# A gated block on one NeuronCore: gate and up of two of four chunks by seven block products in place of eight

## The chip, the cores and the metric

The kernel runs on one core of one Trainium2 chip. Its time is device microseconds of one execution, the median of several runs. The engines have a queue each and work it in order: TensorE (matmuls, in the profile PE, its weight loads PEld), VectorE (DVE), ScalarE (ACT), GpSimd (POOL); SyncE (SP) issues the DMAs. TensorE writes to banks of PSUM, each of 128 partitions by 512 f32 values, and the banks are read by VectorE and ScalarE.

## The reference

For 2048 rows of width 576 (f32):

```python
xn = layernorm(x)
# A: attention, 32 heads of width 18, causal, a window of 256
q, k, v = split(xn @ wqkv)
s = softmax(mask(q @ k.T * 18 ** -0.5)) @ v  @ wo
# B: bilinear gated unit, inner width 4608, no nonlinearity inside
g = silu(((xn @ w_gate) * (xn @ w_up)) @ w_down)
out = x + s * g
```

The kernel keeps f32 accuracy with f16 matmuls: each operand is split into a high and a low f16 part (high = f16(scaled value), low = the rest), and a product is high x high + high x low + low x high.

## The kernel before

**The data.** `XT` holds the normalized x transposed, 128 partitions by nine planes by 2048 columns: planes 0 to 3 are the high parts of the 512 first rows of D, plane 4 the high part of the last 64 rows (partitions 0 to 63) and their low part (64 to 127), planes 5 to 8 the low parts. `XT2` repeats the high part of the last 64 rows in partitions 64 to 127. One tile of weights (`UW[g, k]`, ten planes of 128 x 128) has the high parts of four full blocks and the tail in planes 0 to 4, the low ones in 5 to 9. In plane 4 the 64 last rows stand twice, so that a single pass there gives high x high and high x low of the tail.

**The order of the work.** After a prologue of some 180 us (layernorm, q, k, v) come 72 slots: 18 groups `g` of 256 inner columns (two tiles `ft` of 128), and in each the four chunks `c` of 512 rows. A slot is `sl = 4 * g + c` and has 16 places. In each place TensorE gets a quarter of a gate or up product: gate of ft 0 at places 0 to 3, up of ft 0 at 4 to 7, then ft 1. A product is 13 passes of 512 columns and one half-row pass for low x high of the tail; a gate's and an up's half-row pass run side by side in the two halves of the rows (lines 933 and 934).

All else is put between them by a table written out by hand: `at(slot, place, f, ...)`; a place of 16 or more falls into a later slot. In each place first the matmuls of gate and up are issued (with `gate_out` or `up_out` at the last quarter), then the score matmuls, then the down matmuls, then the rest in the order in which it was put in the table. Each engine works this order as it comes, so an operation that waits holds what stands behind it on its engine.

- **FFN.** `gate_out` (line 773, ScalarE) copies the gate's bank to `gt`, `up_out` (778, VectorE) multiplies the up bank by it into `ht`. `h_hi` (783, ScalarE) and `h_lo` (788, VectorE) split it. `down` (801) is eight groups of six matmuls of 288 columns a slot, each added to `acc` by VectorE (806); the eight take turns on one bank, `dn`, at places 7, 9, 11, 13, 15, 17, 19, 21 after their slot's start plus one slot.
- **Attention**, one pair of heads a slot, in slots 1 to 64. `score_pairs` (678, TensorE, places 3 and 11), `score` (686, VectorE: masks and takes the maximum), line 688 (GpSimd: the bias of the exponential), `probs` (693 and 696, ScalarE: exponential and high part), `turn_probs` (701: the low part, j = 0 on VectorE, j = 1 on GpSimd, and then a DMA transpose from SP, 704), `weigh` (713, TensorE, 37 columns) in the next slot, `finish` (725 to 737, VectorE and GpSimd) and `store_o` (742) every sixteen steps.
- **Weights.** For each group, `ffn_raw` loads the next group's weights; `ffn_amax` takes maxima on VectorE, `ffn_spread_out` and `ffn_spread_in` bring them to all partitions over DRAM, `ffn_scale` makes scales; `up_hi` (147, ScalarE), `up_lo` (150, VectorE) and `dn_hi`, `dn_lo`, `dn_low` (413, GpSimd) make the parts. In steady state chunk 0 has the gate's maxima and two `dnw` parts, chunk 1 the other maxima, chunks 2 and 3 the scale and the parts.

PSUM's eight banks are four `s`, two `up`, one `dn`, one `pv`. A gate and an up bank are allocated together every eight places.

## Time and profile before

| | |
|---|---|
| median of 3 runs | 1644.06 us (1643.51 to 1644.07) |
| the profiled execution's own time | 1644.22 us |
| its span, first to last instruction | 1642.5 us |
| TensorE busy | 1632.9 us, 99% |
| VectorE, ScalarE, GpSimd busy | 1182.4, 912.0, 608.0 us |
| a slot of the steady part | 19.83 us |

In a row of the profile's groups stand line, engine, operation, what it writes and reads by the program's names, its shape and count, then busy time and mean ns of one, then the idle time of the engine ahead of it and what ended it. In the view of busy time by windows, each row is a stretch of the run, with the busy time of every engine. In a timeline a row has start, length, engine, line, operation and count; matmuls are pipelined and their ends modelled, so that their starts tell the rate.

### The profile page before, as it was taken

What the parts mean: (1) busy time and instruction counts of PE and PEld (TensorE: products, weight loads), DVE (VectorE), ACT (ScalarE), POOL (GpSimd) and SP (SyncE); (2) the same over time, 40 slices, a digit from 0 to 9 for tenths busy, and PEclk for the clock granted to TensorE, in tenths of its full rate; (3) what the DMA queues carried; (4) which work ended last, traced back from release to release, by engine and by line L of the source; (5) the groups of instructions that cost most, each with busy time, mean ns of one, the idle gap of its engine ahead of it and who ended that gap; (6) DMA issues with size and microseconds to landing.
All of it is one profiled execution on the core that took longest, in us unless ns stands there. A gap on an engine that the chain in (4) does not pass through costs nothing.

```text
span 1642.5 us, 33722 instructions
## 1 busy us (share of the span) xinstructions
PE 1632.9 (99%) x12330; PEld 931.7 (57%) x12330; DVE 1182.4 (72%) x2993; ACT 912.0 (56%) x1581; POOL 608.0 (37%) x1044
## 2 busy tenths in 40 slices
PE   8999999999999999999999999999999999999999
PEld 5464455555555555555555555555555555555577
DVE  7533577777677878787878787878787877865545
ACT  6431465656565656676666666666666666632230
POOL 3110134434343545454444444444444453511000
PEclk9999999999999999999999999999999999999999
DMA  9571446455556777676767575767665766650228
GB/s 241 160 199 74 127 86 118 97 109 109 107 107 131 144 120 136 113 144 114 142 137 144 109 147 103 152 105 145 139 136 114 142 118 129 129 130 20 60 70 219
DMA packets 531798, 206.37 MB, mean 126 GB/s; under 512 B 470576, under 2 KB 510384, under 8 KB 531632
## 3 DMA queue, kind: packets, MB, share of 16 engines
q1 hardware_dynamic: 531632, 204.21, 60.3%
q8 instruction: 97, 1.59, 0.4%
q14 instruction: 69, 0.57, 0.1%
HBM read 76.63 MB, written 23.75 MB: 61 GB/s over the span
## 4 chain that ended last, share of the span: by engine, by line
PE 97%; DMA 1%; ACT 0%; DVE 0%; issue 0%; POOL 0%; SPq 0%; POOLq 0%; DVEq 0%; ACTq 0%
PE up L930 49%; PE dn L801 24%; PE pv L713 4%; PE s L337 3%; PE up L933 3%; PE s L678 2%; PE s L801 2%; PE s L895 2%; PE up L895 1%; PE up L337 1%; PE s L288 1%; PE pv L337 1%; PE dn L337 1%; DMA xr<-in_A_x_dram 0%; PE up L288 0%
## 5 line engine op out<-in xcount | busy, mean ns | idle before, releaser
L930 PE MATMUL up<-XT,upw 128*128 128x512 f16 x3744 | 926.6, 378 | 0.0
L930 PEld LDWEIGHTS <-upw 128*128 128x128 f16 x3744 | 331.0, 97 | 279.6 <-issue 0.8
L801 PE MATMUL dn<-dnw,hh 128*128 128x288 f16 x3168 | 475.6, 286 | 0.0
L801 PEld LDWEIGHTS <-hh 128*128 128x128 f16 x3456 | 326.2, 98 | 198.9 <-issue 41.1
L806 DVE SCALAR_TENSOR_TENSOR acc<-dn,sc,acc 128x288 f32<-128x288 f32 x496 | 255.9, 516 | 248.9 <-PE dn L801 243.0
L688 POOL TENSOR_SCALAR mx<-mx,sig 128x1 f32<-128x1 f32 x512 | 199.7, 390 | 529.9 <-DVE mx L686 500.0
L713 PEld LDWEIGHTS <-pt 128*128 128x128 f16 x2880 | 138.1, 96 | 57.9
L713 PE MATMUL pv<-vt,pt 128*128 128x37 f16 x2880 | 142.9, 179 | 0.0
L773 ACT ACTIVATE gt<-up 128x512 f32<-128x512 f32 x144 | 85.4, 593 | 83.9 <-PE up L933 80.1
L783 ACT ACTIVATE hh<-ht 128x512 f16<-128x512 f32 x144 | 89.9, 624 | 60.8 <-DVE ht L778 60.8
L778 DVE SCALAR_TENSOR_TENSOR ht<-up,gt 128x512 f32<-128x512 f32 x144 | 99.1, 688 | 21.0 <-PE up L930 8.5
L788 DVE SCALAR_TENSOR_TENSOR hh<-hh,ht 128x512 f16<-128x512 f16 x144 | 98.8, 686 | 0.0
L375 DVE TENSOR_REDUCE am<-raw 128x1 f32<-128x640 f32 (+1 forms) x108 | 85.0, 787 | 0.9 <-DMA raw<-in_B_w_gate_dram 0.9
L413 POOL TENSOR_SCALAR dnw<-dnw 128x576 f16<-128x576 f16 x36 | 69.1, 1919 | 23.1 <-ACT dnw L147 20.4
L147 ACT ACTIVATE upw<-raw,sc 128x640 f16<-128x640 f32 x72 | 59.0, 823 | 23.3 <-DVE sc L126 22.3
L337 PEld LDWEIGHTS <-upw 128*128 128x128 f16 x416 | 40.4, 98 | 49.5 <-issue 1.7
L150 DVE SCALAR_TENSOR_TENSOR upw<-raw,sc,upw 128x640 f16<-128x640 f32 x72 | 62.9, 876 | 0.1
L678 PE MATMUL s<-ks,qs 54*128 54x384 f16 (+2 forms) x512 | 60.2, 312 | 0.0
L933 PE MATMUL up<-XT,upw 64*128 64x512 f16 x144 | 55.7, 387 | 0.0
L934 PE MATMUL up<-XT,upw 64*128 64x512 f16 x144 | 55.7, 387 | 0.0
L895 PEld LDWEIGHTS <-ot 128*128 128x128 f16 x476 | 44.5, 98 | 10.7
L806 DVE SCALAR_TENSOR_TENSOR acc<-s,sc,acc 128x288 f32<-128x288 f32 x48 | 24.6, 517 | 35.4 <-PE s L801 35.3
(2248 smaller groups left out, 2193.6 us busy)
## 6 DMA issues: line engine op xcount, KB each, us to landing
raw<-in_B_w_down_dram SPq DMA_DIRECT2D x36, 288.0 KB
qk_d<-qp SPq DMA_DIRECT2D x18, 512.0 KB
raw<-in_B_w_gate_dram SPq DMA_DIRECT2D x36, 256.0 KB
raw<-in_B_w_up_dram SPq DMA_DIRECT2D x36, 256.0 KB
vt<-v_d SPq DMA_DIRECT2D x48, 111.0 KB
ks<-qk_d SPq DMA_DIRECT2D x96, 54.0 KB
v_d<-vo SPq DMA_DIRECT2D x16, 296.0 KB
xr<-in_A_x_dram SPq DMA_DIRECT2D x16, 288.0 KB
```

Source lines behind the costliest of these rows:

```text
L337: nc.tensor.matmul(ps, a, b, start=i == 0 and not opened, stop=i == 12 and opened)
L678: nc.tensor.matmul(ps[:, :hi_ - lo_], QS[s][r, i * 128:(i + 1) * 128], KS[s][r, lo_:hi_], start=True, stop=True)
L688: nc.gpsimd.tensor_scalar(mx[:, 1:2], mx[:, 0:1], sig[:, 1:2], shift, op0=OP.mult, op1=OP.add)
L713: nc.tensor.matmul(PVB[s][:, j, i, :VW], pt[:, 2 * nb * j + n], VT[s][:, lo_ + n % nb, j * VW:(j + 1) * VW], start=n == 0, stop=n == 2 * n ...
L778: nc.vector.scalar_tensor_tensor(h, ps, U_SC, GT.pop((sl, ft)), op0=OP.mult, op1=OP.mult)
L783: nc.scalar.activation(hh[:, 0], h, AF.Copy, scale=1.0 / LO)
L788: nc.vector.scalar_tensor_tensor(hh[:, 1], hh[:, 0], -LO, h, op0=OP.mult, op1=OP.add)
L801: nc.tensor.matmul(ps[:, :HALF], a, b, start=q == 0, stop=q == len(l) - 1)
L806: nc.vector.scalar_tensor_tensor(d, ps[:, :HALF], SC[g][:, 9:10], d, op0=OP.mult, op1=OP.add)
L895: nc.tensor.matmul(pr[j][:, :cols[j].stop - cols[j].start], a, b[:, cols[j]], start=i == 0, stop=i == 13)
L930: nc.tensor.matmul(banks[up], a, b, start=i == 0 and not up, stop=i == 12 and up == 1)
L933: nc.tensor.matmul(banks[0], *half_pass(w, c, False), start=False, stop=True)
```

## The change

In chunks 0 and 1 of each group from g = 1 on (34 of 72 slots) the gate and up products are computed in another way. The 512 full rows of D, the 256 inner columns of the group and the 512 rows of the chunk make a product of 2 x 2 by 2 x 2 blocks: weights `b[k, f]` (k: half of D, f: inner tile), x's `a(i, j)` (i: half of the chunk's rows, j: half of D). In place of the eight block products there are seven, from sums of x's blocks and sums of weight blocks (the Winograd form of Strassen's scheme). Each is taken with the same three passes of high and low parts, for two blocks of 128 rows each, gate and up side by side in one bank of 2 x 256 columns: 12 matmuls of 256 columns. The tail of 64 rows is added in the products 1, 4, 5 and 6, as 12 more and as four half-row ones (`seven_half`). Product 6 takes a difference of the tails (`XD`).

What is added:

- once, in slots 0 to 2: the sums of x (`s_steps`, `SUMS_AT`), about 13 GpSimd operations for each of the two chunks, with splits on ScalarE and VectorE; block (1, 0) of `XT` is overwritten by one;
- for each group: four sums of weight blocks for the gate and four for the up (`t_sum`, GpSimd), their high parts (`t_hi`, four on ScalarE) and low parts (`t_lo`, four on VectorE);
- for each of the 34 slots: three copies of banks on ScalarE (products 0, 3, 4), four reads with addition on VectorE (1, 2, 5, 6), three sums of 512 on GpSimd, and gate x up as four halves of 256 columns, three on GpSimd, one on VectorE.

In these slots `gate_out` and `up_out` are gone; `h_hi` and `h_lo` go to places 16, 17 and 17, 21. Two of the four j = 0 subtractions of `turn_probs` go from VectorE to GpSimd there. The two `up` banks take the products in turn, seven to a slot.

What is moved: the maxima, `ffn_spread_out`, `ffn_scale`, low parts of up and the `dnw` parts by some places; `finish` one place earlier behind such a slot; `store_o` writes a quarter of the head pairs each fourth step, in two or three DMAs, where it wrote four DMAs each sixteenth. Scales by powers of two change (XS, PROJ, G_SC, U_SC, and FTOP for the FFN weights), and tiles change pools so that the new ones fit: `hh`, `gt`, `ht` and `acc` in one pool in the prologue's memory (`gt` with four buffers, `ht` two), the sums in another, which closes ahead of the last two slots.

```diff
-        return ring.tile([128, 2, 512], F16, name="hh", bufs=4)
+        return post.tile([128, 2, 512], F16, name="hh", bufs=4)
     def f_ring(name):
-        return ring.tile([128, 512], F32, name=name, bufs=1)
+        return post.tile([128, 512], F32, name=name, bufs=4 if name == "gt" else 2)
...
+    SEVEN = (0, 1)
+    def seven(sl):
+        return sl >= NCH and sl % NCH in SEVEN
+    def t_sum(g, kind, pair, i):
...
+        nc.gpsimd.tensor_tensor(t[:, i], x0, x1, op=OP.subtract)
+    def t_hi(g, kind, pair):
...
+        hi(w, TF[g, kind, pair], SC[g][:, 6 + kind:7 + kind])
+    def t_lo(g, kind, pair):
...
+        lo(w[:, :, 1], TF[g, kind, pair], SC[g][:, 6 + kind:7 + kind], w[:, :, 0])
...
+        def split(n, parts):
+            return (lambda: nc.scalar.copy(parts()[0], t[n]),
+                    lambda: nc.vector.tensor_tensor(parts()[1], t[n], parts()[0], op=OP.subtract))
...
+            begin,
+            lambda: do("v", (1, 0, 1), (1, 1, 1), s),
+            lambda: do("u", "u", "v", s),
+            split("u", lambda: part(0)),
+            lambda: do("u", "u", (0, 0, 0), m),
+            lambda: do("u", "u", (0, 0, 1), m),
+            split("u", lambda: part(1)),
...
-        (nc.gpsimd if j else nc.vector).tensor_tensor(pp[:, a + n:a + 2 * n], sm, pp[:, a:a + n], op=OP.subtract)
+        (nc.gpsimd if j or seven(s + 1) and i in (0, 1) else nc.vector).tensor_tensor(pp[:, a + n:a + 2 * n], sm, pp[:, a:a + n], op=OP.subtract)
...
-        at(b, 28, finish, s)
-        if s % 16 == 15:
-            for i in range(4):
-                at(b, 33 + 4 * i, store_o, s // 16, i)
+        at(b, 27 if seven(b) else 28, finish, s)
+        if s % 4 == 3:
+            for part in range(3 if s % 16 == 15 else 2):
+                at(b, 30 + 2 * part, store_o, s // 16, s % 16 // 4, part)
...
-                    at(b, ((9, 13) if g == 1 else (5, 9), (17, 21), (24, 26))[kind][half], ffn_amax, g, kind, half)
-            at(b, 28, ffn_spread_out, g)
+                    at(b, ((9, 13) if g == 1 else (9, 9), (17, 23), (24, 29))[kind][half], ffn_amax, g, kind, half)
+            at(b, 30, ffn_spread_out, g)
             at(b, 34, ffn_spread_in, g)
-            at(b, 41, ffn_scale, g)
-            for k, (ph, pl) in enumerate(((42, 45), (47, 49), (51, 53), (55, 57))):
+            at(b, 40, ffn_scale, g)
+            for k, (ph, pl) in enumerate(((42, 45), (44, 50), (49, 53), (55, 57))):
...
+        if g > 0:
+            for n in range(4):
+                at(b, (38, 39, 40, 41)[n], t_sum, g, 0, n // 2, n % 2)
+                at(b, (51, 51, 53, 54)[n], t_sum, g, 1, n // 2, n % 2)
+            for n in range(4):
+                at(b, (45, 48, 54, 57)[n], t_hi, g, n // 2, n % 2)
+                at(b, (47, 49, 55, 58)[n], t_lo, g, n // 2, n % 2)
-        for k, (ph, pw, pl) in enumerate(((60, 62, 61), (64, 66, 66)) if g else ((64, 65, 66), (68, 69, 70))):
+        for k, (ph, pw, pl) in enumerate(((61, 62, 63), (63, 66, 65)) if g else ((64, 65, 66), (68, 69, 70))):
...
+    SUMS_AT = ((0, 1, 1, 8, 9, 10, 12, 15, 15, 19, 23, 23, 25, 26, 27, 31, 27),
+               (6, 6, 6, 11, 12, 14, 16, 17, 18, 24, 29, 29, 31, 33, 35, 40, 39))
...
+    def seven_unit(g, c, q):
+        for kind in range(2):
+            w1, w2, tw = UW[g, kind], UW[g, 2 + kind], TW[g, kind]
...
+            for n in range(2):
+                for a, b in ((wh, xh), (wh, xl), (wl, xh)):
+                    yield kind, a[:, n], b[:, n]
...
+    def seven_half(g, c):
+        CH[5], CH["n"] = bank("up", 2), 2
+        for kind in range(2):
...
+            nc.tensor.matmul(CH[4][:, o], w[0:64, 9], x[0:64], start=False, stop=kind == 1)
...
+            nc.tensor.matmul(CH[5][:, o], w[64:128, 9], xh, start=kind == 0, stop=False)
...
+    def seven_copy(sl, q, name):
+        nc.scalar.activation(seven_new(sl, name), CH[q], AF.Copy, scale=H_SC)
+    def seven_add(sl, q, x, name):
+        x = SV[sl, x]
+        nc.vector.scalar_tensor_tensor(seven_new(sl, name), CH[q], H_SC, x, op0=OP.mult, op1=OP.add)
+    def seven_sum(sl, x, y, name):
...
+        nc.gpsimd.tensor_tensor(seven_new(sl, name), x, y, op=OP.add)
+    def seven_mult(sl, name, i, f, eng):
...
+        eng.tensor_tensor(HT[sl, f][:, 256 * i:256 * i + 256], u[:, 0:256], u[:, 256:512], op=OP.mult)
+    def seven_place(sl, place):
...
+        n = SEVEN_N[place]
+        for _ in range(n):
+            q, (kind, a, b) = CH["l"].pop(0)
+            if q not in CH:
+                CH[q] = bank("up", 2)
...
+            nc.tensor.matmul(CH[q][:, o], a, b, start=CH["n"] == 0, stop=last and q != 4)
+            CH["n"] += 1
+            if last and q != 4:
+                seven_read(sl, q, place)
+        if place == 11:
+            seven_half(g, c)
+            seven_read(sl, 4, place)
...
+        elif q == 4:
+            seven_copy(sl, 4, "4")
+            at(sl, place + 1, seven_u4, sl)
+            at(sl, place + 3, seven_mult, sl, "4", 1, 1, gp)
+        elif q == 5:
+            seven_add(sl, 5, "3", "11")
+            at(sl, place + 1, seven_mult, sl, "11", 1, 0, gp)
+        else:
+            seven_add(sl, 6, "t", "t")
+            at(sl, place + 1, seven_mult, sl, "t", 0, 1, vec)
...
+    SEVEN_N = (4, 9, 7, 6, 4, 5, 6, 8, 3, 6, 3, 5, 8, 8, 8, 6)
...
+            if sl < NSLOT and seven(sl):
+                seven_place(sl, place)
+            elif sl < NSLOT:
```

189 lines of the change are left out of this document (161 added, 28 removed).

## The prediction

> **What bounds the kernel now.** I read the page first: busy time by engine, the chain that ended last, the groups (count, then busy us and mean ns, then idle before).
>
> ```profile
> PE 1632.9 (99%) x12330; PEld 931.7 (57%) x12330; DVE 1182.4 (72%) x2993; ACT 912.0 (56%) x1581; POOL 608.0 (37%) x1044
> ...
> PE 97%; DMA 1%; ACT 0%; DVE 0%; issue 0%; POOL 0%; SPq 0%; POOLq 0%; DVEq 0%; ACTq 0%
> ...
> L773 ACT ACTIVATE gt<-up 128x512 f32<-128x512 f32 x144 | 85.4, 593 | 83.9 <-PE up L933 80.1
> L783 ACT ACTIVATE hh<-ht 128x512 f16<-128x512 f32 x144 | 89.9, 624 | 60.8 <-DVE ht L778 60.8
> L778 DVE SCALAR_TENSOR_TENSOR ht<-up,gt 128x512 f32<-128x512 f32 x144 | 99.1, 688 | 21.0 <-PE up L930 8.5
> L788 DVE SCALAR_TENSOR_TENSOR hh<-hh,ht 128x512 f16<-128x512 f16 x144 | 98.8, 686 | 0.0
> ...
> L150 DVE SCALAR_TENSOR_TENSOR upw<-raw,sc,upw 128x640 f16<-128x640 f32 x72 | 62.9, 876 | 0.1
> ```
>
> The chain is TensorE's for 97% of the span. So a shorter TensorE program shortens the run, as long as the other queues keep up. How much room they have is read by stage: four neighbouring slots of the steady part (chunks 1, 2, 3, 0), from the view of busy time by windows.
>
> ```profile
> 814.44:834.27 19.83, 19.83 (x163) 11.24 (x161) 15.98 (x42) 11.71 (x20) 7.31 (x15) 1.00 0.75 130
> 834.27:854.10 19.83, 19.83 (x163) 11.23 (x161) 14.65 (x41) 12.42 (x21) 8.32 (x17) 1.00 0.79 152
> 854.10:873.93 19.83, 19.83 (x163) 11.24 (x161) 16.02 (x41) 14.31 (x24) 9.53 (x15) 1.00 0.65 135
> 873.93:893.76 19.83, 19.83 (x163) 11.24 (x161) 16.56 (x42) 12.48 (x21) 11.68 (x18) 1.00 0.80 158
> sum 79.32, PE 79.32 PEld 44.95 DVE 63.20 ACT 50.92 POOL 36.85; mean PE 19.83 PEld 11.24 DVE 15.80 ACT 12.73 POOL 9.21
> ```
>
> Columns after the length: PE, PEld, DVE, ACT, POOL, then the granted clock (1.00, full). A slot takes 19.83 us and TensorE never pauses; VectorE has 16 us a group of four free, GpSimd 42, ScalarE 28.
>
> **TensorE's term.** Its rate is read from starts, since ends are modelled. TensorE's timeline of one slot:
>
> ```profile
> 799.95 1.03 PE L930 MATMUL up<-XT,upw 128*128 128x512 f16 x4
> ...
> 802.50 1.46 PE L930 MATMUL up<-XT,upw 128*128 128x512 f16 x6
> 803.79 0.90 PE L801 MATMUL dn<-dnw,hh 128*128 128x288 f16 x6
> 804.53 1.03 PE L930 MATMUL up<-XT,upw 128*128 128x512 f16 x4
> 805.39 0.31 PE L713 MATMUL pv<-vt,pt 128*128 128x37 f16 x6
> 805.54 0.81 PE L930 MATMUL up<-XT,upw 128*128 128x512 f16 x3
> ...
> 807.08 1.46 PE L930 MATMUL up<-XT,upw 128*128 128x512 f16 x6
> 808.47 0.39 PE L933 MATMUL up<-XT,upw 64*128 64x512 f16 x1
> 808.47 0.39 PE L934 MATMUL up<-XT,upw 64*128 64x512 f16 x1
> 808.69 0.49 PE L678 MATMUL s<-ks,qs 54*128 54x384 f16 x4
> ```
>
> Six of 512 columns: 803.79 - 802.50 = 1.29, 215 ns each. Six of 288: 0.74, 123 ns. Six of 37: 0.15, 25 ns, each with its own 128x128 weights. The line through 512 and 288 gives 0.413 ns a column and 110 ns for 256 columns; half of 215 gives 107.5, the lower end. Six full ones before a half-row pair take 1.39 (807.08 to 808.47), 0.10 more than six alone: the switch of row groups.
>
> A slot now spends on gate and up 52 x 215 = 11.2 us, two half-row pairs 0.43, and two switches 0.2. Changed, it has 96 matmuls of 256 columns (seven products of 12, plus 12 for the tail rows: the sixteen entries of the new place table sum to 96), two pairs of half that length (0.22), and again two switches, one at the pairs, one at the scores of place 3, which lose the pair ahead of them. 96 x 109.5 = 10.5 us. Saved: 11.63 - 10.73 = 0.90 us a slot, or 1.08 if 107.5 holds. I take 0.91 (288 columns is the nearer row). It applies in 17 groups x 2 chunks = 34 slots: 31 us, and 37 at the other end. The slot becomes 18.9 us.
>
> The Trainium skill ("TensorE: Matmul & The Clock Gate", Back-to-back issue gap) gives a gap of N/2.4 + 2.5 ns, 109 ns here, but also says that a stream of weight-load and matmul pairs runs slower, at about 81 ns for N = 128. That speaks against halving the columns: 25 ns on each of 96 would be 2.4 us a slot, more than is saved. The 25 ns row above, weights included, and 123 ns at 288 columns speak for the first formula.
>
> **What the other engines get.** Durations not quoted yet, from the groups of GpSimd and from line 701's instructions (min/median/max in ns, then the start):
>
> ```profile
> L413 POOL TENSOR_SCALAR dnw<-dnw 128x576 f16<-128x576 f16 x36 | 69.1, 1919 | 23.1 <-ACT dnw L147 20.4
> ...
> L219 POOL TENSOR_TENSOR xh<-xn,xh 128x512 f16<-128x512 f32 x15 | 17.4, 1157 | 0.1
> ```
> ```profile
> L701 DVE TENSOR_TENSOR pp<-sm__1937,pp x1: 415/415/415, 200.7 to 200.7; 128x256 f16<-128x256 f32 x1
> L701 POOL TENSOR_TENSOR pp<-sm__1967,pp x1: 668/668/668, 204.9 to 204.9; 128x256 f16<-128x256 f32 x1
> L701 POOL TENSOR_TENSOR pp<-sm__2032,pp x1: 917/917/917, 207.3 to 207.3; 128x384 f16<-128x384 f32 x1
> L701 DVE TENSOR_TENSOR pp<-sm__2020,pp x1: 867/867/867, 207.8 to 207.8; 128x384 f16<-128x384 f32 x1
> L701 DVE TENSOR_TENSOR pp<-sm__2060,pp x1: 546/546/546, 210.1 to 210.1; 128x384 f16<-128x384 f32 x1
> ```
>
> VectorE, a group: eight product reads with addition (like L778, 0.688: 5.5), two 256-wide products (0.415: 0.8), four low parts of summed weights (between L788's 0.686 and L150's 0.876 at 640 columns, 0.70: 2.8); gone are four up reads (2.75) and four subtractions given to GpSimd (0.546: 2.2). Net +4.2: 67.4 of 77.5 us, 87%. Chunk 1 is fullest: 15.98 + 2.75 + 0.4 + 0.7 (two low parts of h land there instead of one) - 1.4 - 1.1 = 17.3 of 18.9.
>
> ScalarE: two more copies (0.593) and four high parts (0.624): 50.9 + 3.7 = 54.6, 70%.
>
> GpSimd: a seven-product slot adds three sums of 512 (1.157), three products of 256 (0.668) and two subtractions (0.917): 7.3 us; chunks 2 and 3 add eight weight sums of 256 (5.3). No row has f32 out of two f32: below, 1.157; above, L413's pace, 1919/576 x 512 = 1.71 us for 512. I take 1.157, the row of the same operation. Group: 36.85 + 14.6 + 5.3 = 56.8, 73%. But chunk 0 holds 11.68 + 7.3 = 19.0 of 18.9 us: full, with a carry into chunk 1 (7.31 + 7.3 = 14.6), which drains it.
>
> **Where a lag reaches TensorE.** Before, a gate or up bank had four places, nearly 5 us, to be read. Now both `up` banks turn over seven times a slot, so a read must end within the next product. The tightest is product 1 in chunk 0. VectorE meets the down matmuls of place 3 and then has four operations:
>
> ```profile
> 800.15 0.52 DVE L806 SCALAR_TENSOR_TENSOR acc<-dn,sc,acc 128x288 f32<-128x288 f32 x1 [0.32 <-PE dn L801]
> 800.58 0.55 DVE L686 CUSTOM_DVE_ANT_0 sm__11141<-s,bias 128x384 f32<-128x384 f32 x1
> 801.06 0.08 DVE L686 DVE_READ_ACCUMULATOR2_ANT mx<- 128x1 f32 x1
> 801.06 0.69 DVE L788 SCALAR_TENSOR_TENSOR hh<-hh,ht 128x512 f16<-128x512 f16 x1
> 801.66 0.55 DVE L686 CUSTOM_DVE_ANT_0 sm__11159<-s,bias 128x384 f32<-128x384 f32 x1
> ```
>
> Accumulation 0.43, score 0.48, low part of h 0.60 (start to start), then the read, 0.69 until its bank is free. Ahead of them stands the landing of the down matmuls: TensorE starts the next stretch at 799.95 and VectorE its accumulation at 800.15, 0.20 later. Together 2.4 us. TensorE meanwhile issues 14 matmuls (1.53), one down (0.74) and 12 of 37 columns (0.31): 2.58 us. It fits by 0.2. The other turnovers have more: product 2 in chunk 1 has two low parts of h around it and still 0.9 us by the same counting, and the one `dn` bank, read by VectorE before the next down, keeps 0.25 at place 5 of chunk 0, where the read of product 1 has pushed the accumulation back. VectorE's two-input operations also stretch: line 701's 867 ns at 207.8 runs beside GpSimd's 917 at 207.3, and 546 alone.
>
> The second place is longer. Chunk 0's last GpSimd product (place 14) stands behind the finish copies, a subtraction, two sums and small ones: about 5.8 us after VectorE's finish at 15.7 us, so 2.5 us into chunk 1. ScalarE's high part of h waits for it and holds the copy of the new product 0 behind it, done at 3.6; its bank is wanted at 5.4. Cover: 1.8 us. The h rows themselves are wanted only from place 7.
>
> So I charge few waits: from 0 to 0.5 us a slot, 0.1 taken, 3 us in all. Nothing excludes a loss beyond that, see the rivals. The one-off sums of x cost more at the start: some 20 GpSimd operations of 1.157 us fall into slots 0 and 1, about 23 us beside the scores' own, and VectorE's and ScalarE's splits wait for them in order. Slot 0 has no attention or down work, some 12 us, so GpSimd enters slot 1 several us late; bounds 0 and 8 us, 3 taken. **What is moved.** The stores of o (2 or 3 each fourth step, where there were 4 each sixteenth) go on SP at places 14, 16 and 18 after finish, behind GpSimd's casts there; the probability transposes and key loads behind them have 4 places or more until their use, so I charge nothing, and a late weighing if GpSimd lags. The spread of the weight maxima leaves two places later and is read one place earlier: it passes VectorE's and SP's queues with three places less between, behind the first stores and a transpose; what its landing would hold is VectorE's scale in chunk 2, where the banks still have four places: nothing. The amax reductions, low parts and dnw splits that change places are the same instructions on the same queue, counted above where a slot gets one more or fewer; the subtractions (L701, j = 0) leave VectorE's queue for GpSimd's, where they stand ahead of the later mx rows, and ScalarE's exponentials wait for those: this is the lag priced as the second place above. The scales, pools and the memory that tiles share change no duration; the first `gt` lies where the prologue's tiles were and may wait a store there, inside the one-off bound.
>
> The profiled execution took 1644.22 us for a span of 1642.5; the runs' median is 1644.06, the same. **1644.2 - 31 + 3 + 3 = 1619 us.**
>
> **Rivals.** (A) As above, 1610 to 1628. (B) The thin covers give way by half a microsecond a slot: 34 x 0.5 = 17, so 1644 - 31 + 17 + 4 = 1634. For it: 0.2 us of cover and VectorE at 92% in chunk 1. Against: the low parts and reads show no stretching, only L701's kind does. (C) The other side: GpSimd's all-f32 sums are slow and chunk 0 overflows. With x us for 512 columns, its work is 11.68 + 1.83 + 4.5x + 0.3; it breaks the cover above 18.9 + 1.8 = 20.7, and the gain of two slots (1.8) is gone at 22.5, x = 1.93. At 2.1 us: 23.3, 2.6 a group, 17 x 2.6 = 44: 1644 - 31 + 44 + 3 = 1660. For it: L413 is a slow GpSimd row; against: GpSimd's two-tensor rows give (917 - 668)/128 = 1.95 and (1157 - 917)/128 = 1.9 ns an element, with 0.18 us fixed. "GPSIMD Engine Reference" (Performance versus the Vector engine) of the Trainium skill has 4497 ns for an f32 sum of 2048, an estimate of 1.2 us here; no row shows it. (D) The weight loads show at 256 columns: 25 ns (the row of 37 columns) on top, 34 x (2.4 - 0.9) = 51, 1695. The 288 row speaks against.
>
> **Numbers.** A 0.62, B 0.20, C 0.13, D 0.01, and 0.04 for waits that eat just the gain. Faster 0.82, same 0.04, slower 0.14; 0.2% (3 us) is about what runs tell apart. The range, 1609 to 1640, holds A and B; A alone is 1610 to 1628.
>
> **What would show it.** Starts 109 ns apart in a product; chunk 0 and 1 slots of 18.9 us, the others 19.8; GpSimd sums near 1.16 us; no idle before the first matmul of products 2 and 3. Wrong if TensorE sits idle for `up` reads of VectorE, if GpSimd's sums are over 1.9 us, or if slots 0 to 2 lose over 8 us.

## The result and the profile after

The changed kernel takes 1655.98 us (median of 4 runs, 1652.49 to 1657.87) against 1644.07 us before: ratio 1.0071, 95% interval 1.0053 to 1.0088, so **0.7% slower** where a gain was forecast, 1619 us in a range of 1609 to 1640. The profiled execution took 1652.49 us for a span of 1650.8 us; the one before 1644.22 for 1642.5. So the traces have 8.3 us of loss to explain; the other three executions of the changed kernel took 3.3 to 5.4 us longer than the profiled one, and no trace shows where.

Lines of the page of the kernel after: busy time, the chain that ended last by engine and by line, and groups.

```profile
PE 1614.9 (98%) x13826; PEld 1078.7 (65%) x13826; DVE 1303.2 (79%) x3111; ACT 970.3 (59%) x1693; POOL 1003.1 (61%) x1468
...
PE 67%; DVE 19%; POOL 6%; issue 5%; ACT 1%; DMA 1%; SPq 0%; DVEq 0%; POOLq 0%; ACTq 0%
...
L1015 POOL TENSOR_TENSOR gt<-gt 128x512 f32<-128x512 f32 x102 | 129.6, 1271 | 13.0 <-ACT gt L1007 5.3
...
L154 DVE SCALAR_TENSOR_TENSOR tw<-tf,sc,tw 128x512 f16<-128x512 f32 x68 | 68.7, 1010 | 33.4 <-POOL tf L426 25.7
```

TensorE is busy for 18 us less, yet the chain is TensorE's for 67% of the span instead of 97%: VectorE and GpSimd stand in it for a quarter. The low parts of the summed weights, forecast at 0.70 us, average 1.01, and 25.7 us of VectorE's idle time ahead of them wait for GpSimd's weight sums (L426).

What TensorE itself waits for in the kernel after (us in total, times, longest), the rows that matter:

```profile
PE s L783 <- DVE mx L791: 10.7, 12, 0.9
PE dn L908 <- DVE acc L913: 8.1, 27, 0.4
PE up L1187 <- DVE ht L885: 3.0, 1, 3.0
```

Twelve waits of 0.9 us are one in each of groups 4 to 15, 3.0 us a single event. Where they lie is read by stage. The kernel after, busy time by windows, one for each slot (chunks 1, 2, 3, 0) of the same group as in the prediction; columns: length, PE, PEld, DVE, ACT, POOL, clock.

```profile
820.93:839.96 19.03, 19.03 (x207) 15.52 (x205) 16.92 (x42) 12.23 (x22) 15.74 (x23) 1.00 0.81 139
839.96:859.81 19.85, 19.85 (x162) 11.23 (x160) 16.85 (x43) 12.83 (x23) 15.58 (x25) 1.00 0.66 125
859.81:881.93 22.12, 20.51 (x162) 11.29 (x160) 19.94 (x47) 15.95 (x28) 11.43 (x18) 1.00 0.55 104
881.93:900.80 18.87, 18.87 (x206) 15.55 (x204) 15.73 (x39) 13.10 (x23) 15.93 (x23) 1.00 0.75 157
sum 79.87, PE 78.26 PEld 53.59 DVE 69.44 ACT 54.10 POOL 58.69; mean PE 19.57 PEld 13.40 DVE 17.36 ACT 13.53 POOL 14.67
```

The two slots with seven products take 18.87 and 19.03 us, the gain that was forecast; the profile shows no idle time of TensorE in them. **Chunk 3, which still has eight products, takes 22.12 us in place of 19.83**, with VectorE busy for 19.94 of it.

Slot lengths, counted from the first gate or up matmul of one slot to that of the next, worked out from both traces (difference after minus before, us):

```
                     slots 1-3   chunk 0  chunk 1  chunk 2  chunk 3
median, groups 5-15      -        -0.96    -0.80    +0.03    +2.29
sum, groups 1-17       +8.35     -16.5    -13.2     +0.5    +29.7
slot 1 alone           +7.36 (16.25 to 23.61)
```

With 0.6 us less before the first slot they add up to the 8.3 us. Chunk 3's loss is 0.75 us in groups 1 to 3, where some scores are narrower, 2.28 to 2.30 in groups 4 to 15, and nothing in group 16, whose slot has the same weight sums and low parts but no scores any more (VectorE is busy there for 11.89 us only). So there are two losses to explain: chunk 3 (30 us) and the start (8 us).

**Chunk 3.** One stretch of the timeline of the kernel after, GpSimd, ScalarE, VectorE (line 154 makes low parts, line 791 the scores' maxima) and TensorE (start, duration, instruction, idle before it and its releaser):

```profile
867.36 0.64 POOL L793 TENSOR_SCALAR mx<-mx,sig 128x1 f32<-128x1 f32 x1 [2.98 <-DVE mx L791]
868.08 0.73 POOL L426 TENSOR_TENSOR tf<-raw 128x256 f32<-128x256 f32 x1
868.88 1.27 POOL L426 TENSOR_TENSOR tf<-raw,tf 128x256 f32<-128x256 f32 x1
870.11 0.91 POOL L806 TENSOR_TENSOR pp<-sm__13204,pp 128x384 f16<-128x384 f32 x1
871.12 0.55 POOL L793 TENSOR_SCALAR mx<-mx,sig 128x1 f32<-128x1 f32 x1
...
871.70 0.71 ACT L798 ACTIVATE sm__13282<-sm__13282,mx,sig 128x384 f32<-128x384 f32 x1 [2.41 <-POOL mx L793]
872.44 0.51 ACT L801 CAST pp<-sm__13282 128x384 f16<-128x384 f32 x1
872.86 0.72 ACT L151 ACTIVATE tw<-tf,sc 128x512 f16<-128x512 f32 x1
...
868.26 0.08 DVE L791 DVE_READ_ACCUMULATOR2_ANT mx<- 128x1 f32 x1
870.99 0.54 DVE L806 TENSOR_TENSOR pp<-sm__13261,pp 128x384 f16<-128x384 f32 x1
873.68 1.38 DVE L154 SCALAR_TENSOR_TENSOR tw<-tf,sc,tw 128x512 f16<-128x512 f32 x1 [2.15 <-POOL tf L426]
...
874.21 0.49 PE L783 MATMUL s<-ks,qs 54*128 54x384 f16 x3
875.59 0.32 PE L783 MATMUL s<-ks,qs 54*128 54x384 f16 x1 [0.90 <-DVE mx L791]
```

The same scores of TensorE in the kernel before, and the down product behind them:

```profile
868.17 0.49 PE L678 MATMUL s<-ks,qs 54*128 54x384 f16 x4
868.59 0.91 PE L801 MATMUL dn<-dnw,hh 128*128 128x288 f16 x6
```

VectorE wrote the second score's maximum at 868.3, but two weight sums and a subtraction stand ahead of its scaling (mx) in GpSimd's queue, until 871.12. ScalarE's exponential waits 2.41 us for that scaling, in order ahead of the high part of the summed weights; VectorE's low part, in order ahead of the next scores, waits 2.15 us for the high part; and TensorE's next scores wait 0.90 us for VectorE. The row names GpSimd's sum as releaser, but the sums were done at 870.1; the late one is the high part of 872.86.

By TensorE's starts the 2.29 us stand in three places. The down product behind these scores starts 1.81 us after their first matmul (876.02), 0.42 before: 1.39 us. The slot's last down product comes another 0.60 us later: VectorE is at work without a break from that low part on and reaches the accumulation ahead of it late. Its first down product is 0.32 us later, which is another matter and comes up again below.

**The start.** The kernel after in slot 1 (window), the sums of x by group, and what ScalarE and VectorE wait for in that slot (sx: the high and low parts of the sums):

```profile
190.28:213.89 23.61, 18.78 (x95) 8.80 (x94) 19.50 (x34) 11.74 (x22) 21.74 (x24) 0.93 0.17 48
```
```profile
L460 POOL TENSOR_TENSOR tw<-XT 128x512 f32<-128x512 f16 x8 | 9.9, 1253 | 0.2
L460 POOL TENSOR_TENSOR tw<-tw 128x512 f32<-128x512 f32 x4 | 5.5, 1367 | 0.3
L460 POOL TENSOR_TENSOR tw<-tw,XT 128x512 f32<-128x512 f32 x4 | 5.2, 1319 | 0.2
```
```profile
ACT sx L463 <- POOL tw L460: 7.6, 3, 3.5
DVE sx L464 <- ACT sx L463: 4.4, 3, 3.0
```

GpSimd is busy for 21.74 of 23.61 us, in a slot that took 16.25 before; the splits on ScalarE and VectorE wait for its sums in order, and TensorE's single wait of 3.0 us, for an `up` bank, lies here. The granted clock, the last figure but two of the row, averages 0.93 in this slot (1.00 before), and TensorE's busy time is 18.78 us (16.25 before). How much of the 7.36 us is the clock and how much the waits, no run separates.

### The profile page after: what moved, and what is told of

The parts are those of the page before. It is cut to its first block, busy times and chain, and to the rows that moved or that the text cites. A ratio compares the mean times of both kernels' runs of the same rounds, so it can differ in the third digit from the quotient of the medians.

```text
span 1650.8 us, 37424 instructions
## 1 busy us (share of the span) xinstructions
PE 1614.9 (98%) x13826; PEld 1078.7 (65%) x13826; DVE 1303.2 (79%) x3111; ACT 970.3 (59%) x1693; POOL 1003.1 (61%) x1468
## 4 chain that ended last, share of the span: by engine, by line
PE 67%; DVE 19%; POOL 6%; issue 5%; ACT 1%; DMA 1%; SPq 0%; DVEq 0%; POOLq 0%; ACTq 0%
PE up L1036 20%; PE dn L908 17%; PE up L1183 11%; DVE acc L913 4%; PE s L341 3%; PE pv L818 3%; DVE tw L154 3%; PE s L908 2%; DVE upw L154 2%; PE s L783 2%; DVE hh L895 2%; PE s L1146 2%; POOL tf L426 2%; PE up L1146 1%; PE up L341 1%
## 5 line engine op out<-in xcount | busy, mean ns | idle before, releaser
L1183 PE MATMUL up<-XT,upw 128*128 128x512 f16 x1976 | 489.0, 379 | 0.0
L1183 PEld LDWEIGHTS <-upw 128*128 128x128 f16 x1976 | 175.9, 97 | 151.3 <-issue 2.8
L1036 PEld LDWEIGHTS <-upw 128*128 128x128 f16 x1632 | 154.6, 98 | 20.0
L1036 PEld LDWEIGHTS <-tw 128*128 128x128 f16 x1632 | 147.0, 97 | 16.9 <-issue 0.3
L1036 PE MATMUL up<-XT,upw 128*128 128x256 f16 x1088 | 150.5, 272 | 0.0
L1015 POOL TENSOR_TENSOR gt<-gt 128x512 f32<-128x512 f32 x102 | 129.6, 1271 | 13.0 <-ACT gt L1007 5.3
L1036 PE MATMUL up<-sx,tw 128*128 128x256 f16 x816 | 115.4, 271 | 0.1
L1011 DVE SCALAR_TENSOR_TENSOR gt<-up,gt 128x512 f32<-128x512 f32 x136 | 93.1, 684 | 26.9 <-POOL gt L1015 24.8
L1036 PE MATMUL up<-XT,tw 128*128 128x256 f16 x816 | 105.6, 272 | 0.0
L154 DVE SCALAR_TENSOR_TENSOR tw<-tf,sc,tw 128x512 f16<-128x512 f32 x68 | 68.7, 1010 | 33.4 <-POOL tf L426 25.7
L1021 POOL TENSOR_TENSOR ht<-gt 128x256 f32<-128x256 f32 x102 | 79.0, 788 | 17.5 <-DVE gt L1011 12.3
```

Source lines behind the costliest of these rows:

```text
L154: nc.vector.scalar_tensor_tensor(w, rv, s, h, op0=OP.mult, op1=OP.subtract)
L1011: nc.vector.scalar_tensor_tensor(seven_new(sl, name), CH[q], H_SC, x, op0=OP.mult, op1=OP.add)
L1015: nc.gpsimd.tensor_tensor(seven_new(sl, name), x, y, op=OP.add)
L1036: nc.tensor.matmul(CH[q][:, o], a, b, start=CH["n"] == 0, stop=last and q != 4)
L1183: nc.tensor.matmul(banks[up], a, b, start=i == 0 and not up, stop=i == 12 and up == 1)
```

## Experiments

Theories: **W**, a wait (GpSimd's order in chunk 3); **V**, VectorE simply has too much work in chunk 3; **C**, contention (VectorE's operations last longer beside GpSimd's); **O**, the one-off sums of x. All lengths are compared with before, as above. The first four kernels have one execution each.

**Low parts left out**

```
-        lo(w[:, :, 1], TF[g, kind, pair], ...)
+        pass        # and the matmuls read the high part twice
```

> Leaves out the low parts of the summed weights (the four t_lo a group; the high part is used in their place, so the output is not the reference's). In the trace of the changed kernel the slots of chunk 3 take 22.1 us in place of 19.83, 2.29 more, in 13 groups, and that is 29.7 us in all. Theory W (a wait: VectorE stands 2.15 us in chunk 3 for the high part of summed weights, which ScalarE makes late because GpSimd's weight sums stand ahead of its mx rows) and theory V (work: VectorE is simply too full in chunk 3, 19.94 us busy) both expect chunk 3 back at 19.8 to 20.0 and about 28 us less than the changed kernel, 1624 to 1630. A theory by which the sums on GpSimd or the high parts on ScalarE alone hold TensorE up expects chunk 3 to stay above 21.

1631.87 us; chunk 3 +0.32 (20.15), slot 1 +7.43. Without the low parts nothing on VectorE waits for the sums, and nearly all of chunk 3's loss is gone. Both W and V would have it so, and the time is just above their 1624 to 1630. (The summed products lack their low parts here.)

**Weight sums left out**

```
-        nc.gpsimd.tensor_tensor(t[:, i], x0, x1, op=OP.subtract)
+        TF[g, kind, pair] = (the raw blocks)     # no sum; high and low parts are still made
```

> Leaves out the eight weight sums a group on GpSimd (the high and low parts are made from blocks of the raw weights instead, with the same shapes, so the output is not the reference's). W expects the wait for the high part gone and chunk 3 at 20.2 or less: about 25 us under the changed kernel, near 1630. V expects VectorE's work unchanged, its low parts at most less stretched, and chunk 3 still above 21: 1645 or more.

1629.63 us. Chunk 3 in this kernel, by window:

```profile
1007.26:1027.40 20.14, 19.98 (x163) 11.23 (x161) 20.00 (x47) 15.94 (x28) 8.64 (x14) 1.00 0.58 113
```

The products are of raw blocks here, of the same shapes. All of VectorE's instructions are there (47, as after), and chunk 3 has lost only 0.31 us. So V falls as the main cause: the same work fits 20.14 us. About 2 of the 2.29 us come from GpSimd's sums. By itself this doesn't tell W from C.

**Low parts of the up half later (64 and 66 for 55 and 58)**

```
-                at(b, (47, 49, 55, 58)[n], t_lo, g, n // 2, n % 2)
+                at(b, (47, 49, 64, 66)[n], t_lo, g, n // 2, n % 2)
```

> The low parts of the up half of the summed weights go from places 55 and 58 (chunk 3, places 7 and 10) to 64 and 66 (chunk 0, places 0 and 2); nothing else changes, and the output is the reference's. V: chunk 3 loses 1.4 to 2.1 us of VectorE's work, which chunk 0 can take (15.7 of 18.9 us busy): chunk 3 near 20.0, chunk 0 at most 0.5 longer, about 22 us less, 1627 to 1637. W: the wait of VectorE goes too, since by place 64 the high part is long there; the same time. If both are wrong, chunk 3 stays at 22.

1645.37 us: chunk 3 +0.43, chunk 0 +0.27 in place of -0.96. The wait is out of chunk 3, but chunk 0, which was to lose 0.5 us at most, loses 1.23 of its gain: the low parts stand in VectorE's queue there. Both theories had 1627 to 1637 and missed.

**Seven products from the second pair of groups on**

```
-        return sl >= NCH and sl % NCH in SEVEN
+        return sl >= 2 * NCH and sl % NCH in SEVEN
-    SUMS_AT = ((0, 1, 1, 8, 9, ...
+    SUMS_AT = ((20, 23, 26, 29, 33, ...     # over slots 1 to 6
```

> Seven products from group 2 on, not from group 1 (32 slots, not 34), and the sums of x spread over slots 1 to 6 where they stood in slots 0 to 2. Theory O (slot 1's 7.36 us and the 1.0 of slots 2 and 3 are GpSimd's sums of x, packed into slots 0 and 1) expects slot 1 back near 16.3, slots 2 to 6 longer by at most 0.5 together, and the gain of two slots (1.6 us) lost: 5 to 7 us under the changed kernel. The other reading (slot 1 waits for the new places of the tiles, or for the prologue's stores) expects slot 1 still over 20 us. Chunk 3 stays at 22.1 from group 4 on in both.

1654.75 us. Slot 1 is back to 16.25, but slots 3 and 4 lose 3.86 and 1.87: the loss moved with the sums of x, which supports O, yet these places gained little: 5 to 7 us were expected, and 1654.75 lies among the executions of the change as made. Chunk 3 is unchanged (+2.30), as it should be.

**Weight sums of the up half earlier (49 to 50)**

```
-                at(b, (51, 51, 53, 54)[n], t_sum, g, 1, n // 2, n % 2)
+                at(b, (49, 50, 50, 50)[n], t_sum, g, 1, n // 2, n % 2)
```

> Nothing is left out: the four sums of the up half of the weights go from places 51, 51, 53, 54 (behind the first mx row of chunk 3's scores on GpSimd) to 49, 50, 50, 50, ahead of it, where GpSimd stood idle for 2.98 us in the changed kernel. W says that it is their place in GpSimd's queue, not their work, that costs: chunk 3 falls to about 20.2, as without the sums (20.14), the rest stays, and the time is 17 x 2 x 0.9 (13 full groups) less, 1627 to 1632. A theory by which GpSimd's work itself, or VectorE's port shared with it, is the cost expects chunk 3 at 21 or more, 1640 and up.

1648.39 us (ratio 1.0024, 1.0015 to 1.0034). Chunk 3's window and two of VectorE's rows in it:

```profile
1019.46:1040.81 21.35, 20.43 (x163) 11.21 (x161) 21.14 (x47) 15.93 (x28) 12.55 (x18) 1.00 0.53 108
```
```profile
1024.00 0.74 DVE L154 SCALAR_TENSOR_TENSOR tw<-tf,sc,tw 128x512 f16<-128x512 f32 x1
1024.66 1.08 DVE L806 TENSOR_TENSOR pp<-sm__15896,pp 128x384 f16<-128x384 f32 x1
```

The wait of 2.15 us is down to 0.2, but chunk 3 still loses 1.52: VectorE is now busy for 21.14 us with the same 47 instructions, because some last longer (the subtraction 1.08 us, 0.54 alone). Durations added up one by one give 24.35 us here, 23.10 without the sums, 23.14 after. So the move exchanged W's wait for C's stretch, and W's forecast (20.2, 1627 to 1632) missed; the contention reading had 21 or more and 1640 and up. In the change as made, though, the sums add nothing to VectorE's durations on balance (23.14 against 23.10): there it is the wait that costs.

**Early sums, and the sums of x at every second place of slots 1, 2, 4 and 5**

> The early weight sums, and seven products from group 2 on (32 slots), with chunk 0's sums of x at every second place of slots 1 and 2 and chunk 1's at every second place of slots 4 and 5, so that none falls into slot 3, where the weights' parts are made (there the earlier spreading paid 3.86 us). Theory O expects slots 1 to 6 longer by 2 us at most together, where the changed kernel pays 8.4 and the earlier spreading 6.3: with 1.6 us of gain given up, 4 to 5 us less than the early sums alone, 1622 to 1627. If the sums of x cost the same wherever they stand, no gain on the early sums alone.

1642.75 us (0.9987, 0.9978 to 0.9996): just faster than before. Slots 1 to 3 lose 0.75 us instead of 8.35. O holds: the start's loss is the sums of x and goes when they are spread, 5.6 us under the early sums alone (4 to 5 expected). Chunk 3 stays at +1.52, and so the 1622 to 1627, which counted on the early sums, is missed.

**The same, with one of VectorE's subtractions in chunk 3 given to GpSimd**

```
-        (nc.gpsimd if j or seven(s + 1) and i in (0, 1) else nc.vector).tensor_tensor(...)
+        (nc.gpsimd if j or seven(s + 1) and i in (0, 1) or s > 6 and s % 4 == 2 and i == 1 else nc.vector).tensor_tensor(...)
```

> As before it, and one more j = 0 subtraction of chunk 3 (i = 1) on GpSimd in place of VectorE. Theory V in its rest: without the sums chunk 3 still took 20.14 us with VectorE busy 20.00 of them, so the last 0.3 us are VectorE's work. It expects chunk 3 at 19.9 (0.55 us of work less), 13 x 0.25 = 3 us under the kernel ahead. If it is another late wait of GpSimd's (the subtraction stands ahead of mx rows there), chunk 3 gets longer.

1645.73 us (1.0012, 1.0001 to 1.0022). Chunk 3's window:

```profile
1013.99:1035.53 21.54, 20.43 (x162) 11.20 (x160) 21.33 (x46) 15.94 (x28) 14.10 (x19) 1.00 0.57 106
```

One instruction fewer on VectorE (46), and VectorE is busy *longer* (21.33 against 21.14) and chunk 3 longer by 0.19 us, where V expected 19.9. VectorE's idle time is 0.21 us in both, so it is no late wait either. That is C against V: what GpSimd gains is taken from VectorE.

**The whole gate and up weight work 4 and 6 places earlier**

```
-            for k, (ph, pl) in enumerate(((42, 45), (44, 50), (49, 53), (55, 57))):
+            for k, (ph, pl) in enumerate(((38, 41), (40, 46), (45, 49), (51, 53))):   # and so all its steps
```

> From the kernel with the sums of x late (seven products from group 2 on). Every step of the next group's gate and up weights, from the raw loads and the maxima to the scale, the parts and the sums, four places earlier, the sums of the up half at 48, 48, 49, 49; the steps of the down weights stay. Theory C (VectorE is full in chunk 3, because the low parts all stand there and GpSimd's work beside them stretches them: 0.74 us alone, 1.15 to 1.40 beside it) says that work must leave chunk 3: one low part of weights and two of summed weights go to chunk 2, where VectorE is busy 16.9 of 19.86 us. It expects chunk 3 at 20.0 to 20.4 (from 21.35), chunk 2 at most 20.2, and 10 to 18 us under the early sums with late sums of x: 1625 to 1633. If VectorE's fill is not the bound there, chunk 3 stays at 21.3.

> The same by six places, with the sums of the up half at 46, 46, 47, 47. Theory C expects chunk 3 lower still (19.9) and chunk 2 fuller, 20.2 to 20.8: the sum about as with four places, 1623 to 1635. If chunk 2 has the room that its busy time shows, it is a little faster than four places.

1690.72 us (1.028, 1.0262 to 1.0297) and 1721.7 us (1.0469, 1.0453 to 1.0485): misses. What TensorE waits for, first with 4, then with 6 places:

```profile
PE dn L908 <- DVE acc L913: 33.8, 71, 1.1
PE up L1036 <- DVE gt L1011: 8.0, 23, 0.5
```
```profile
PE dn L908 <- DVE acc L913: 63.3, 76, 1.9
PE up L1036 <- DVE gt L1011: 22.9, 30, 1.2
```

The waits feared in the prediction appear: the one `dn` bank and the `up` banks of the seven products, not read in time. Of the 8.0 and 22.9 us of waits for `up`, 5.7 and 17.8 lie in chunk 0; those for `dn` lie in chunks 1 to 3, with six places 41.5 of 63.3 in chunk 2. Against before, chunks 0 to 3 differ by -0.08, +0.49, +1.33 and +1.31 us with four places, by +0.38, +0.57, +3.18 and +0.82 with six. C's forecast fails too: chunk 3 was to fall to 20.0 to 20.4 and 19.9, and took 21.14 and 20.64, with VectorE busy for only 18.61 and 18.04 us of it. As these kernels have waits in all chunks, they do not tell what chunk 3's cause is in the others.

**Low parts of the up half at 60 and 63; the same with late sums of x; low parts at 62 and 65 with late sums of x**

```
-                at(b, (47, 49, 55, 58)[n], t_lo, g, n // 2, n % 2)
+                at(b, (47, 49, 60, 63)[n], t_lo, g, n // 2, n % 2)     # third kernel: 62, 65
```

The late sums of x stand in slots 1 and 2 and in slots 4 to 6, with seven products from group 2 on.

> The low parts of the up half's summed weights stand at places 60 and 63 in place of 55 and 58; the weight sums stay where the change put them, and all the rest too. The wait theory (in chunk 3 VectorE's 2.15 us of idle ahead of the low parts are the loss, because GpSimd's sums hold the maxima rows, these ScalarE's exponentials, these the high parts): VectorE has other work until the parts are there, the wait is under 0.5 us, and, as the sums stay off VectorE's stretch of unbroken work, nothing is stretched: chunk 3 20.2 to 20.6 us, chunk 0 18.9 to 19.3, in all 1656 - 17 x 1.6 = 1629, from 1624 to 1635; slot 1 still loses 7.4. The contention theory (GpSimd's sums cost chunk 3 about 1.3 us wherever they stand beside VectorE's work): chunk 3 21.0 to 21.5, in all 1640 to 1648. The chunk 0 rival (the late parts take their 1.5 us out of chunk 0's VectorE, as the parts at 64 and 66 did): chunk 3 20.3 but chunk 0 19.6 to 20, 1640 to 1646.

> As the kernel with the low parts at 60 and 63, with seven products only from the second pair of groups on (32 slots in place of 34, which gives back about 1.8 us) and the sums of x spread over the later half of slots 1 and 2 and of slots 4 and 5. The one-off theory (slot 1's 7.4 us come from the sums of x that stand in GpSimd's queue ahead of the scores' rows): slots 1 to 7 lose under 3 us in all, so the time is the first kernel's less 8.4, plus 1.8 and 1 to 3: 4 to 6 us below it, 1624 if that is 1629. If slot 1's loss has another cause, it stays at 7 and the time is 1 to 2 us above the first kernel's.

> As the second kernel of this set, with the low parts at 62 and 65, two places later. Wait theory: the wait is gone at 60 and 63 already or is down to a few tenths, so this gains chunk 3 at most 0.3 us a group; chunk 0 rival: the later parts push VectorE's reads at chunk 0's start, chunk 0 longer by 0.2 to 0.5 us. Net from 3 us faster to 8 us slower than the second kernel: 1621 to 1632.

1645.18 us (1.0004, 0.9995 to 1.0013), 1640.14 us (0.9975, 0.9966 to 0.9984) and 1635.87 us (0.9947, 0.9932 to 0.9962). Chunk 3 loses 1.10, 1.10 and 0.43 us; chunk 0 gains 0.96, 0.96 and 0.26; slots 1 to 3 lose 8.43, 0.10 and 0.25. The late sums of x take the start's loss away, as O had it: the second kernel lies 5 us under the first, 8.3 less at the start and some 2 given back with two slots of seven products, the rest by single delays. W expected chunk 3 at 20.2 to 20.6 with 60 and 63; it was 20.92, and the first kernel's time lies in the range of the contention theory (1640 to 1648). A wait of 1.17 us had come up one step on, for the next block of weights, whose high part stands behind the same late exponential on ScalarE. The late maximum was still there. The third kernel gained 4.3 us on the second, more than either theory allowed (3): chunk 3 gave 0.67 us a group, not 0.3.

**The sums behind the second score's maximum (52, 52, 56, 56 for 51, 51, 53, 54)**

```
-                at(b, (51, 51, 53, 54)[n], t_sum, g, 1, n // 2, n % 2)
+                at(b, (52, 52, 56, 56)[n], t_sum, g, 1, n // 2, n % 2)
-                at(b, (45, 48, 54, 57)[n], t_hi, g, n // 2, n % 2)
+                at(b, (45, 48, 56, 59)[n], t_hi, g, n // 2, n % 2)
```

> As the kernel with the low parts at 62 and 65 and the late sums of x, but the up half's weight sums stand at places 52, 52, 56, 56 (behind the maximum of chunk 3's second score, which they stood ahead of) and their high parts at 56 and 59. Wait theory: the maximum of the second score no longer stands 3.7 us in GpSimd's queue, ScalarE's exponential behind it starts 2 to 3 us earlier, and VectorE's last wait in chunk 3 (1.17 us for the high part of the last upw block) goes: chunk 3 from 20.26 to 19.85-20.05, 13 x 0.3 = 4 us, in all 1630 to 1634. If VectorE's work alone sets the rest (18.2 us busy of 20.26), chunk 3 stays at 20.2 and the time at 1636; if the sums there stretch VectorE's two-input operations again, chunk 3 is 20.5 to 21.2 and the time 1639 to 1648.

**1630.01 us, ratio 0.9908 (0.9891 to 0.9924): the fastest of those that leave nothing out, 0.9% faster than before and 1.6% than the change as made.** GpSimd in the same part of chunk 3 as above, and chunk 3's window:

```profile
1011.87 0.64 POOL L793 TENSOR_SCALAR mx<-mx,sig 128x1 f32<-128x1 f32 x1 [2.99 <-DVE mx L791]
1012.59 0.92 POOL L806 TENSOR_TENSOR pp<-sm__15794,pp 128x384 f16<-128x384 f32 x1
1013.60 0.72 POOL L793 TENSOR_SCALAR mx<-mx,sig 128x1 f32<-128x1 f32 x1
1014.40 0.73 POOL L426 TENSOR_TENSOR tf<-raw 128x256 f32<-128x256 f32 x1
1015.21 0.73 POOL L426 TENSOR_TENSOR tf<-raw,tf 128x256 f32<-128x256 f32 x1
```
```profile
1004.33:1024.47 20.14, 19.99 (x163) 11.23 (x160) 18.62 (x45) 16.05 (x28) 12.31 (x19) 1.00 0.60 114
```

The second mx starts 1.73 us after the first (3.76 after the change), the wait of 1.17 us is gone, and chunk 3 is at +0.31; all the work is done, with one of the two low parts now in chunk 0 (45 of VectorE's 47 instructions are left in chunk 3). The time is in W's range, chunk 3 a little above it (19.85 to 20.05). But in chunk 3 this kernel differs from the change as made in two ways at once. The low parts at 62 and 65 alone had brought chunk 3 from +2.29 to +0.43, because VectorE no longer stands waiting ahead of the next scores; the order of the sums brought the 0.12 from there, and 0.26 in chunk 0, which gains 0.52 now instead of 0.96 after the change. Sums behind the maximum with the low parts where the change had them were not run. So W's chain is shown by the trace, by the kernels that leave out the sums or the low parts, and by the later low parts. What the order on GpSimd is worth by itself is measured only with the low parts already late.

**Neither sums nor low parts of the up half**

```
-                at(b, (51, 51, 53, 54)[n], t_sum, g, 1, n // 2, n % 2)
-                at(b, (47, 49, 62, 65)[n], t_lo, g, n // 2, n % 2)
+                if n < 2:
+                    at(b, (47, 49)[n], t_lo, g, n // 2, n % 2)
```

> As the kernel with the low parts at 62 and 65 and the late sums of x, with the up half's weight sums and the low parts of these sums left out (the raw blocks stand for the sums, the high parts for the low ones), so that the output is another. If the two causes are the whole difference: chunk 3 19.83 to 19.90, chunks 0 and 1 18.87 and 19.03, 0.9 us gained in each of 32 slots, 28 us, less 1 to 2 for the sums of x: 1616 to 1620, the forecast. If something else in the change costs, it stays above 1624.

1622.74 us (0.987, 0.9855 to 0.9885), a little above the 1616 to 1620 expected. The raw blocks stand for the up half's sums, and its products read the high part twice. Lengths: chunk 0 -0.96, chunk 1 -0.81, chunk 3 still +0.31. This 0.31 is neither the sums nor the low parts of the up half. VectorE and GpSimd at the end of chunk 2 of this kernel:

```profile
1001.02 1.53 DVE L154 SCALAR_TENSOR_TENSOR upw<-raw,sc,upw 128x640 f16<-128x640 f32 x1
...
999.57 0.95 POOL L840 TENSOR_TENSOR ob<-o,ob 128x144 f16<-128x144 f32 x1
1000.61 0.27 POOL L794 TENSOR_SCALAR mx<-mx,sig 128x1 f32<-128x1 f32 x1
1000.96 0.92 POOL L807 TENSOR_TENSOR pp<-sm__15549,pp 128x384 f16<-128x384 f32 x1
```

The low part of an ordinary block, 0.88 us before the change, takes 1.53: it started 0.06 us after GpSimd's subtraction. The accumulation behind it is late, and TensorE's first down product of chunk 3, which waits for that, starts 0.96 us after the matmuls ahead of it, not 0.64. The same place in the kernel before:

```profile
852.98 0.88 DVE L150 SCALAR_TENSOR_TENSOR upw<-raw,sc,upw 128x640 f16<-128x640 f32 x1
...
853.04 1.59 POOL L701 TENSOR_TENSOR pp<-sm__11833,pp 128x384 f16<-128x384 f32 x1
```

There VectorE started 0.06 us ahead of GpSimd, and GpSimd's subtraction was the one that took longer. The same pair, 1.53 us and a first down product 0.32 late, stands in the kernel after and in those without low parts and without sums; no run changes it alone. Of the 10 us between this profiled execution and the forecast without its 6 us of waits and sums (1613), chunk 3 has 4.2, chunk 1 2.5 (most of it single delays), and two slots that keep eight products 1.8.

**The sums behind the maximum, low parts at 60 and 63**

> As the kernel with the sums behind the second maximum, with the low parts at 60 and 63 in place of 62 and 65, into VectorE's two waits for down matmuls (0.33 and 1.16 us) in chunk 3. If the low part at 65 costs chunk 0 its 0.5 us: chunk 0 back to 18.9, chunk 3 20.14 to 20.4, 16 x 0.5 less up to 13 x 0.25: 2 to 8 us faster, 1622 to 1628. If the parts' inputs are late there (the high part of the second pair now stands at 59 on ScalarE), a wait comes back: chunk 3 20.4 to 21 and no gain, 1629 to 1634.

1631.21 us (0.9919, 0.9903 to 0.9936), no gain: chunk 0 is back to -0.96 in most groups, so the low part at 65 was its loss, but chunk 3 goes to +0.72 (20.55), as the second reading had it. With the low parts at 60 and 63 the order of the sums is worth 0.38 us of chunk 3 (1.10 before). One microsecond of VectorE's work fits neither slot for nothing.

## Why the prediction was wrong

**The step that failed** is the one on what the other engines get: VectorE's and GpSimd's room was summed over a group (67.4 of 77.5 us, 56.8) and walked through only for chunks 0 and 1, where the products change. The weight sums were priced as 5.3 us of GpSimd's time in chunks 2 and 3 and never set into the queue, and chunk 3 was never looked at. The totals are nearly right (VectorE 69.4 measured, GpSimd 58.7), and say nothing: two sums ahead of one small scaling, with a low part that VectorE waits for ahead of the next scores, cost TensorE 2 us a group. "[T]his is the lag priced as the second place above" was said of the moved subtractions, in chunks 0 and 1; the same sentence on the weight sums would have found chunk 3.

In the forecast's own sum, 1644.2 - 31 + 3 + 3, the terms measured are -29.7 for the matmuls, +30.2 for the waits in the slots behind the start (chunk 3 alone 29.7) and +8.35 for the start, with 0.6 us less ahead of it: 1652.5.

Point by point:

- TensorE's term: forecast 0.91 us a slot; measured 0.96 and 0.80, and 29.7 us over all slots of chunks 0 and 1 against 31. Of the 0.16 that chunk 1 gains less, 0.13 stand at its first down product. The 256-column matmuls run as the line through 512 and 288 said. In TensorE's timeline of the kernel after, nine of them start at 802.65 and the next matmul at 803.63, 109 ns each:

```profile
802.65 1.14 PE L1036 MATMUL up<-XT,upw 128*128 128x256 f16 x9
803.63 0.90 PE L908 MATMUL dn<-dnw,hh 128*128 128x288 f16 x6
```

- GpSimd's share by chunk: chunk 0 was called full, 19.0 of 18.9 us; it holds 15.93, and chunk 2 has 15.58. The total was right, its place was not.
- Rival D (weight loads show at 256 columns) is out by the same rows.
- Rival C (slow sums of 512 on GpSimd): they took 1.271 us against 1.157 taken and 1.93 needed for harm. Out in its mechanism, though its sign was right: the loss came from GpSimd, by the order and not by the size.
- The two tight places of chunks 0 and 1 (0.2 and 1.8 us of cover) held: the profile shows TensorE busy for the whole of those slots. So rival B is out as described. With the weight work four and six places earlier, reads in chunk 0 were late at once.
- "The low parts and reads show no stretching, only L701's kind does" was read off the trace of before and was wrong: of the low parts of up weights and of h (224), 4 started there with more than 0.15 us of a two-tensor operation of GpSimd's to go, after the change 60. Even before, one such part took 1.41 us, and three of 36 `dnw` parts 1.2 to 1.3 for 0.81. The 0.32 us a group at chunk 3's first down product come from this. The term low parts of summed weights, 0.70 us, measured 1.01; ordinary low parts went from 0.876 to 1.006.
- The one-off sums: 3 us forecast, 8 as the bound, 8.35 measured in slots 1 to 3. The count was 20 operations at 1.157, 23 us; there are 20 whole ones at 1.25 to 1.49 us and 6 small ones, 31 us by the groups. Slots 0 to 2 lost 7.9, just under the 8 that were to make the prediction wrong; but without chunk 3's 29.7 us the kernel would still have been 21 us faster than before.
- Of the three signs that were to tell, no idle for `up` reads in the seven products and GpSimd's sums under 1.9 us spoke for the forecast. None of the three looked at chunk 3. The forecast of 19.8 us for the slots that keep eight products did, and it failed there.
- What is moved: the stores, transposes and the spread of maxima show no wait of TensorE's beyond 0.2 us in the kernel after: nothing was charged, and that was right.

## What to carry to other kernels

An engine with a quarter of its time free still delays the chain if a new operation stands ahead of a small one that others wait for: set each added instruction into its in-order queue, and name the next instruction behind it and who waits for that, in *every* stage it lands in, above all in those that the change does not speak of. When a wait is removed, look one step on before counting the gain (here 60 and 63 only handed it to the next block). Look for the second half of the chain as well: two sums just ahead of a small urgent operation cost 2 us a group where another engine's work stood waiting in order behind it, and 0.4 us or less once that work had been put later.

## What the runs showed of the hardware

VectorE and GpSimd exclude one another for some operations. From the trace after, VectorE's operations by kind (count; shortest, median, mean, longest, ns):

```
ht  <- up (PSUM), gt          x76    678   682   684    692
gt  <- up (PSUM), gt          x136   674   685   684    693
acc <- dn (PSUM), acc         x496   497   508   510    520
tw  <- tf, tw                 x68    735   744  1010   1403
upw <- raw, upw               x72    868   874  1006   1535
hh  <- hh, ht                 x144   673   685   719   1643
```

Those of the table that read PSUM never stretch; those with two inputs in SBUF do. Of the tw, upw, dnw and hh operations, the ones that started while a two-tensor operation of GpSimd's still had 0.75 to 0.9 us to go took 0.66 us longer (median of 40), with 0.15 to 0.3 to go 0.045 us longer, with under 0.15 none: the remaining time less 0.1 to 0.2. So the later one waits until the earlier is nearly through, and whichever starts first wins: that is the exchange of 1.53 and 0.88 us above, decided by 0.06 us. In the trace after this adds some 57 us to the durations of five kinds of VectorE's operations (count times mean less the undisturbed duration: tw 68 x 0.275, 256-wide products 34 x 0.384, upw 72 x 0.136, dnw 36 x 0.264, hh 144 x 0.038). The Trainium skill ("SBUF — State Buffer", SBUF: two separate sides) states an exclusive lock between GpSimd and VectorE operations with two SBUF inputs, held for the whole instruction; the trace agrees, but for the last 0.1 to 0.2 us.
